# Transposes of probabilities two groups behind the scores, and a weight's conversion in three successive steps

## The chip, the core and the metric

The kernel runs on one core of a Trainium2 chip. The core has a matrix engine (TensorE, PE in the profile), a vector engine (DVE), an activation engine (ACT), GpSimd (POOL) and a queue engine that issues transfers (SyncE, SP). Each has its own queue of instructions, whose order is fixed when the program is built. The metric is the device time of one execution in microseconds, less is better.

## The reference

Attention over a window and a few sink positions, then two feed-forward blocks on its output.

```python
scores = scale * np.matmul(q, k.transpose(0, 1, 3, 2))       # q, k, v: (2, 8, 768, 64)
keep = is_sink | in_window                                   # 4 sinks, window of 128
a = softmax(np.where(keep, scores, -1000000000.0))
x = np.matmul(a, v)                                          # -> (1536, 512)
...
x = (silu(x @ w_gate) * (x @ w_val)) @ w_out                 # 512 -> 1536 -> 512
h = x @ w_in
return (np.maximum(h, 0) + alpha * np.minimum(h, 0)) @ w_out2   # 512 -> 2048 -> 512
```

The weights come as 64-bit floats, everything else that is large as 32-bit floats.

## The kernel before

Attention works on 24 groups. A group is a pair of heads and two blocks of 128 query rows. For a group there are these stages (class Group):

- prep (L213): PE transposes keys and queries, ACT copies them to `th`.
- scores (L248): four matmuls into `ps_s`, a masked pass with row maximum on DVE (L271, from the first group with sink columns on with a copy before it, L269), four exponentials on ACT (L275) that also add up the row sums.
- norm (L288): `rinv`, two small DVE operations (L291, L292), then POOL multiplies the probabilities `pr` by it (L298).
- flip (L310): PE transposes the probabilities into `ps_p` (L320), ACT or DVE copies them to `pt`.
- values (L336): PE multiplies with v into `xp` (L351), ACT and DVE split the result into a high part `xh` (L847) and a low part `xl` (L848), which the first feed-forward block reads.

The function attention (L376) writes the stages of different groups one behind the other. In iteration x it writes scores of group x, values of x - 2, flip of x - 1, norm of x, prep of x + 2, and the loads of x + 3. After each piece it yields a cost.

The feed-forward products need 32-bit weights as a high and a low part. The class Stream loads raw weights (L559, three buffers) and converts them, one at a call of tick (L609). A conversion (L574) is a copy on ACT into `w_m` (L587), three bit operations on DVE (L589, L592, L595), the high part `wh` on ACT (L604) and the low part `wl` = `w_m` - `wh` on DVE (L605).

The function fast (L817) drives both. Until 8 groups have their values it ticks once after each flip, up to six weights. After that, for every 2300 of summed cost, it runs one piece of the first feed-forward block on the first 512 rows and ticks once. Twelve weights have room while attention runs.

The order on DVE during attention is the order in which the program is written. The order on PE, ACT, POOL and SyncE is made by a scheduler from its own estimate of times, so moving a stage in attention moves instructions on all of them.

```python
for x in range(n + 2):
    if x < n:
        for t in range(NG):
            groups[x].scores(t)
    if x >= 2:
        for c in groups[x - 2].values():
            yield c, None
```

Of the kernel before, what the change touches and what calls it, by code (L numbers as in the profile page):

```python
# [7 lines left out]
F32 = mybir.dt.float32  # L8
# [3 lines left out]
AF = mybir.ActivationFunctionType  # L12
ALU = mybir.AluOpType
# [3 lines left out]
P = 128  # L17
# [3 lines left out]
KD = DM // P  # L21
# [14 lines left out]
WX = 7  # L36
RB = 3
VB = 3
ORDER = ((0, 3), (1, 2), (4, 5))
EARLY = 6  # L40
WEAVE = 2300
# [98 lines left out]
class Group:  # L140
    def __init__(self, nc, g, q, k, v, b, hp, i0, put, cs, blk):
        self.nc, self.g, self.q, self.k, self.v = nc, g, q, k, v
        self.b, self.hp, self.i0, self.put = b, hp, i0, put
        self.cs, self.blk = cs, blk
        self.h0 = 2 * hp
        self.j0 = max(0, i0 - 1)
        self.nk = i0 + NG - self.j0
        self.sink = i0 + NG > 2
        self.off = 1 if i0 == 0 else 0
        self.before = self.lead = None  # L150
        if self.sink:
            self.kpos = [0, P, P + KW]
            self.spos = 2 * P
            self.qpos = [P + 2 * KW, P + 3 * KW]
        else:
            self.kpos = [0, P]
            self.qpos = [2 * P, 3 * P]
# [35 lines left out]
    def load_v(self):  # L193
        nc, p = self.nc, self.g.raw_p
        b, h0, j0, nk = self.b, self.h0, self.j0, self.nk
        if self.i0 == 0:
            self.vt = self.wide(self.v, "vr", VB) if self.lead is None else self.lead.vt
            o = 0 if self.lead is None else 2
            self.vr = [[self.vt[:, t, o + e] for e in range(2)] for t in range(nk)]
            return  # L200
        vr = p.tile([P, NG, 4, D], F32, tag="vr", name="vr", bufs=VB).rearrange("p t h d -> p (t h d)")
        vr = vr[:, :NK * 2 * D].rearrange("p (t e d) -> p t e d", e=2, d=D)
# [173 lines left out]
def attention(groups, begin):  # L376
    n = len(groups)

    def stage(f, x):
        if x < n:  # L380
            return getattr(groups[x], f)()

    stage("load", 0)
    begin[0]()
    stage("load_v", 0)
    stage("load", 1)
    stage("load", 2)
    begin[1]()
    for x in range(2):
        for c in groups[x].prep():  # L390
            yield c, None
    for x in range(n + 2):
        if x < n:
            for t in range(NG):
                groups[x].scores(t)
            yield 1200, None
        if x >= 2:
            for c in groups[x - 2].values():
                yield c, None
            yield 0, groups[x - 2]  # L400
        if 1 <= x <= n:
            for t in range(NG):
                groups[x - 1].flip(t)
            yield 1000, None
        if x < n:
            groups[x].norm()
            yield 0, None
        if x + 2 < n:
            for c in groups[x + 2].prep():
                yield c, None  # L410
        stage("load", x + 3)
        stage("load_v", x + 1)
        if x in (2, 4):
            begin[2](x // 2 - 1)
# [131 lines left out]
def big(g, dt, name):  # L546
    return g.x_p.tile([P, KD, T], dt, tag="x", name=name)


class Stream:  # L550
    def __init__(self, nc, g, seq):
        self.nc, self.g, self.seq = nc, g, seq
        self.n_load = self.n_conv = self.n_done = 0
        self.raw, self.w, self.home = {}, {}, {}

    def room(self):
# [14 lines left out]
        self.raw[i] = raw  # L571
        self.n_load += 1

    def convert(self):  # L574
        nc, g, i = self.nc, self.g, self.n_conv
        kind, src, f, scale, slot = self.seq[i]
        rv = self.raw.pop(i).rearrange("p (c t) -> p c t", t=2)
        lo, hi = rv[:, :, 0], rv[:, :, 1]
        m = g.raw_w.tile([P, KD * P], F32, tag="m", name="w_m")
        mi, mu = m.bitcast(I32), m.bitcast(U32)  # L580
        if slot is None or g.exact:
            nc.scalar.activation(m, hi.bitcast(F32), AF.Copy, scale=scale)
            nc.vector.tensor_scalar(out=m, in0=m, scalar1=WMAX, scalar2=-WMAX, op0=ALU.min, op1=ALU.max)
            w2 = g.w2_p.tile([P, KD * P], F32, tag="w2", name="w_2")
            sign, wi = mi, w2.bitcast(I32)
        else:
            nc.scalar.activation(m, hi.bitcast(F32), AF.Abs, scale=scale, accum_out=g.wsum[:, slot:slot + 1])  # L587
            sign, wi = hi, mi
        nc.vector.tensor_scalar(  # L589
            out=wi, in0=mi, scalar1=3, scalar2=0x7FFFFFF8, op0=ALU.logical_shift_left, op1=ALU.bitwise_and  # L590
        )
        nc.vector.scalar_tensor_tensor(  # L592
            out=mi, in0=sign, scalar=-(2**31), in1=wi, op0=ALU.bitwise_and, op1=ALU.bitwise_or
        )
        nc.vector.scalar_tensor_tensor(  # L595
            out=mu, in0=lo.bitcast(U32), scalar=29, in1=mu, op0=ALU.logical_shift_right, op1=ALU.bitwise_or
        )
        w32 = m
        home = next(h for h in g.w_ps if h[1])
        home[1] -= 1  # L600
        self.home[i] = home
        wh = home[0].tile([P, KD * P], F32R, tag="wh", name="wh")
        wl = home[0].tile([P, KD * P], F32R, tag="wl", name="wl")
        nc.scalar.activation(wh, w32, AF.Copy)  # L604
        nc.vector.tensor_tensor(out=wl, in0=w32, in1=wh, op=ALU.subtract)  # L605
        self.w[i] = (wh, wl)
        self.n_conv += 1

    def tick(self, ahead=RB):  # L609
        n = len(self.seq)  # L610
        if self.n_conv < n and self.room() and self.n_load > self.n_conv:
            self.convert()
        while self.n_load < n and self.n_load < self.n_conv + ahead:
            self.load()

    def get(self, i):
        while self.n_conv <= i:
            assert self.room(), (i, self.n_conv, self.n_done)
            if self.n_load <= self.n_conv:
                self.load()  # L620
            self.convert()
        return self.w[i]

    def done(self, n=1):
# [186 lines left out]
def moe(nc, g, st, xs, out, halves):  # L811
    ys = []
    m1 = Moe1(nc, g, st, 0, xs, lambda *y: ys.append(y))
    return m1, Moe2(nc, g, st, 3 * NF1, ys, out, halves)


def fast(nc, tc, ctx, g, n_sink, window, alpha, q, k, v, w_gate, w_val, w_out, x2_in, x2_out, out):  # L817
# [4 lines left out]
    xs = [(big(g, F32R, "xh"), big(g, F32R, "xl")) for _ in range(NPASS)]  # L822
    m1, m2 = moe(nc, g, st, xs, out, [[blk * NG * P for blk in pair] for pair in ORDER])

# [14 lines left out]
    with ExitStack() as inner:  # L839
# [3 lines left out]
        def put(n, half):  # L843
            xh, xl = xs[n]

            def split(src, hp, ts):
                nc.scalar.activation(xh[:, hp, ts], src, AF.Copy)  # L847
                nc.vector.tensor_tensor(out=xl[:, hp, ts], in0=src, in1=xh[:, hp, ts], op=ALU.subtract)  # L848

            return split  # L850

        groups = [
            Group(nc, g, q, k, v, blk // 3, hp, NG * (blk % 3), put(n, half), BLKS[half], blk)
            for n, pair in enumerate(ORDER) for hp in range(NPAIR) for half, blk in enumerate(pair)
        ]
# [89 lines left out]
```

## Time and profile before

| what | value |
|---|---|
| median of three runs | 693.28 us (691.6 to 694.32) |
| the profiled execution's own time | 694.07 us |
| its span, first to last instruction | 692.3 us |
| TensorE busy | 663.5 us, 96% |
| DVE busy | 409.4 us, 59% |
| ACT busy | 302.6 us, 44% |
| POOL busy | 43.0 us, 6% |
| chain of work that ended last, by engine | PE 85%, DVE 5%, ACT 3% |

The span is what the trace covers; the 1.8 us that the execution's own time has beyond it lie around it. Busy shares are averages over the whole span: attention and the feed-forward blocks load the engines differently, so the stretches have to be read one at a time. A number in brackets at the end of a timeline row is the time that the engine stood idle just before this instruction, with what released it.

### The profile page before, as it was taken

The numbers are of one execution on the slowest core, as the hardware profiler recorded it, in microseconds if no ns is written. First come the engines' busy times: TensorE is split into PE (matmuls) and PEld (weight loads), VectorE is DVE, ScalarE is ACT, GpSimd is POOL, SyncE is SP. The second block draws the span as 40 slices with busy tenths as digits, with TensorE's granted clock in tenths as the row PEclk, the third lists the DMA queues.
The fourth block names the chain that finished last, engine by engine and source line by source line (L and its number), as shares of the span: only waits on it lengthen the run. The fifth ranks groups of instructions, "written<-read, shape, count | busy, mean of one in ns | idle before, by whom it ended". The sixth has DMA issues, their size and how long they took to land.

```text
span 692.3 us, 8940 instructions
## 1 busy us (share of the span) xinstructions
PE 663.5 (96%) x3195; PEld 529.6 (76%) x3195; DVE 409.4 (59%) x925; ACT 302.6 (44%) x686; POOL 43.0 (6%) x82
## 2 busy tenths in 40 slices
PE   5769999999999999999999999999999999999996
PEld 2547767677678888888888888888888888888885
DVE  4677778855569862279642489537933753333432
ACT  4877545667356631155322356436611532113320
POOL 2232013311200000000000000000000000000000
PEclk9879999999999999999999999999999999999999
DMA  8764444421025540025400033301500000000111
GB/s 163 172 182 109 121 138 109 101 57 24 12 62 181 183 153 0 1 61 183 123 0 1 0 122 121 123 1 46 167 30 1 1 0 1 0 1 1 61 62 65
DMA packets 76276, 50.87 MB, mean 73 GB/s; under 512 B 50624, under 2 KB 71104, under 8 KB 76224
## 3 DMA queue, kind: packets, MB, share of 16 engines
q1 hardware_dynamic: 73872, 50.22, 25.5%
q8 instruction: 27, 0.44, 0.3%
q10 hardware_dynamic: 2352, 0.01, 0.2%
q14 instruction: 25, 0.20, 0.1%
HBM read 47.07 MB, written 3.15 MB: 73 GB/s over the span
## 4 chain that ended last, share of the span: by engine, by line
PE 85%; DVE 5%; ACT 3%; SPq 3%; issue 1%; DMA 1%; POOL 1%; DVEq 0%; ACTq 0%; POOLq 0%
PE ph L657 6%; PE pf L781 6%; PE ph L655 6%; PE pf L779 6%; PE pf L780 6%; PE ph L656 6%; PE po L723 5%; PE po L725 5%; PE po L724 5%; PE pg L655 4%; PE pv L655 4%; PE pg L656 4%; PE pg L657 4%; PE pv L657 4%; PE pv L656 4%; PE xp L351 2%
## 5 line engine op out<-in xcount | busy, mean ns | idle before, releaser
L668 ACT ACTIVATE hh<-hid 128x512 fp32r<-128x512 f32 x84 | 52.9, 630 | 66.4 <-DVE hid L707 37.2
L669 DVE TENSOR_TENSOR hl<-hid,hh 128x512 fp32r<-128x512 f32 x84 | 57.9, 689 | 35.0 <-ACT hh L668 34.8
L655 PE MATMUL ph<-yh,wh 128*128 128x512 f32 x192 | 74.8, 389 | 0.0
L657 PE MATMUL ph<-yh,wl 128*128 128x512 f32 x192 | 74.7, 389 | 0.0
L656 PE MATMUL ph<-yl,wh 128*128 128x512 f32 x192 | 74.7, 389 | 0.0
L779 PE MATMUL pf<-wh,hh 128*128 128x512 f32 x192 | 74.7, 389 | 0.0
L780 PE MATMUL pf<-wl,hh 128*128 128x512 f32 x192 | 74.7, 389 | 0.0
L761 ACT ACTIVATE neg<-ph,sal 128x512 f32<-128x512 f32 x48 | 33.0, 687 | 93.4 <-PE ph L657 93.4
L781 PE MATMUL pf<-wh,hl 128*128 128x512 f32 x192 | 72.1, 389 | 0.0
L604 ACT ACTIVATE wh<-w_m 128x512 fp32r<-128x512 f32 x68 | 42.6, 630 | 57.3 <-DVE w_m L595 16.9
L605 DVE TENSOR_TENSOR wl<-w_m,wh 128x512 fp32r<-128x512 f32 x68 | 46.4, 687 | 34.8 <-ACT wh L604 34.8
L763 DVE SCALAR_TENSOR_TENSOR hid<-ph,sig,neg 128x512 f32<-128x512 f32 x48 | 36.0, 749 | 38.4 <-ACT neg L761 38.0
L655 PE MATMUL pg<-xh,wh 128*128 128x512 f32 x144 | 56.8, 397 | 0.0
L723 PE MATMUL po<-hh,wh 128*128 128x512 f32 x144 | 56.7, 396 | 0.0
L655 PE MATMUL pv<-xh,wh 128*128 128x512 f32 x144 | 56.5, 392 | 0.0
L657 PE MATMUL pv<-xh,wl 128*128 128x512 f32 x144 | 56.1, 389 | 0.0
L656 PE MATMUL pv<-xl,wh 128*128 128x512 f32 x144 | 56.0, 389 | 0.0
L656 PE MATMUL pg<-xl,wh 128*128 128x512 f32 x144 | 56.0, 390 | 0.0
L657 PE MATMUL pg<-xh,wl 128*128 128x512 f32 x144 | 56.0, 390 | 0.0
L724 PE MATMUL po<-hh,wl 128*128 128x512 f32 x144 | 55.9, 389 | 0.0
L786 DVE TENSOR_TENSOR acc<-pf,acc 128x512 f32<-128x512 f32 x36 | 23.2, 686 | 52.0 <-PE pf L781 52.0
L725 PE MATMUL po<-hl,wh 128*128 128x512 f32 x144 | 52.4, 391 | 0.0
(122 smaller groups left out, 1203.5 us busy)
## 6 DMA issues: line engine op xcount, KB each, us to landing
w_raw<-in_moe_w_out SPq DMA_DIRECT2D x28, 512.0 KB, 3.3
w_raw<-in_moe_w_in SPq DMA_DIRECT2D x16, 512.0 KB, 3.8
w_raw<-in_moe_w_gate SPq DMA_DIRECT2D x12, 512.0 KB, 3.8
w_raw<-in_moe_w_val SPq DMA_DIRECT2D x12, 512.0 KB, 4.4
vr<-in_v SPq DMA_DIRECT2D x32, 96.0 KB, 2.2
out<-acc SPq DMA_DIRECT2D x12, 256.0 KB, 2.3
qr<-in_q SPq DMA_DIRECT2D x32, 64.0 KB, 2.2
kr<-in_k SPq DMA_DIRECT2D x16, 96.0 KB, 2.2
```

Source lines behind the costliest of these rows:

```text
L605: nc.vector.tensor_tensor(out=wl, in0=w32, in1=wh, op=ALU.subtract)
L655: nc.tensor.matmul(ps, wh[:, c], xh[:, kk], start=(kk == 0), stop=False)
L656: nc.tensor.matmul(ps, wh[:, c], xl[:, kk], start=False, stop=False)
L657: nc.tensor.matmul(ps, wl[:, c], xh[:, kk], start=False, stop=(kk == KD - 1))
L668: nc.scalar.activation(hh, hid, AF.Copy)
L669: nc.vector.tensor_tensor(out=hl, in0=hid, in1=hh, op=ALU.subtract)
L723: nc.tensor.matmul(ps, wh[:, mc], hh, start=(x == 0), stop=False)
L724: nc.tensor.matmul(ps, wl[:, mc], hh, start=False, stop=False)
L725: nc.tensor.matmul(ps, wh[:, mc], hl, start=False, stop=(x == CHUNK - 1))
L779: nc.tensor.matmul(ps, hh[:, ts], wh, start=(x == 0), stop=False)
L780: nc.tensor.matmul(ps, hh[:, ts], wl, start=False, stop=False)
L781: nc.tensor.matmul(ps, hl[:, ts], wh, start=False, stop=(x == CHUNK - 1))
```

## The change

The distance between scores and flip becomes a constant, LAG = 2 in place of 1. In iteration x the program now writes scores of group x, values of x - 3, flip of x - 2, norm of x, prep of x + 2. The conversion is cut in three: start (the copy on ACT), bits (the three bit operations and wh), low (wl). One tick does low of one weight, bits of the next and start of the one after it. A weight is counted as converted when its bits are written, and can be used when low is written.

```diff
--- before.py
+++ after.py
@@ -36,6 +36,7 @@
 WX = 7
 RB = 3
 VB = 3
+LAG = 2
 ORDER = ((0, 3), (1, 2), (4, 5))
 EARLY = 6
 WEAVE = 2300
@@ -389,18 +390,18 @@
     for x in range(2):
         for c in groups[x].prep():
             yield c, None
-    for x in range(n + 2):
+    for x in range(n + LAG + 1):
         if x < n:
             for t in range(NG):
                 groups[x].scores(t)
             yield 1200, None
-        if x >= 2:
-            for c in groups[x - 2].values():
+        if x > LAG:
+            for c in groups[x - LAG - 1].values():
                 yield c, None
-            yield 0, groups[x - 2]
-        if 1 <= x <= n:
+            yield 0, groups[x - LAG - 1]
+        if LAG <= x < n + LAG:
             for t in range(NG):
-                groups[x - 1].flip(t)
+                groups[x - LAG].flip(t)
             yield 1000, None
         if x < n:
             groups[x].norm()
@@ -550,7 +551,8 @@
 class Stream:
     def __init__(self, nc, g, seq):
         self.nc, self.g, self.seq = nc, g, seq
-        self.n_load = self.n_conv = self.n_done = 0
+        self.n_load = self.n_start = self.n_conv = self.n_done = 0
+        self.begun = self.halves = None
         self.raw, self.w, self.home = {}, {}, {}
 
     def room(self):
@@ -571,20 +573,30 @@
         self.raw[i] = raw
         self.n_load += 1
 
-    def convert(self):
-        nc, g, i = self.nc, self.g, self.n_conv
+    def start(self):
+        nc, g, i = self.nc, self.g, self.n_start
         kind, src, f, scale, slot = self.seq[i]
         rv = self.raw.pop(i).rearrange("p (c t) -> p c t", t=2)
+        hi = rv[:, :, 1].bitcast(F32)
+        m = g.raw_w.tile([P, KD * P], F32, tag="m", name="w_m")
+        if slot is None or g.exact:
+            nc.scalar.activation(m, hi, AF.Copy, scale=scale)
+        else:
+            nc.scalar.activation(m, hi, AF.Abs, scale=scale, accum_out=g.wsum[:, slot:slot + 1])
+        self.begun = (i, rv, m)
+        self.n_start += 1
+
+    def bits(self):
+        nc, g = self.nc, self.g
+        (i, rv, m), self.begun = self.begun, None
+        kind, src, f, scale, slot = self.seq[i]
         lo, hi = rv[:, :, 0], rv[:, :, 1]
-        m = g.raw_w.tile([P, KD * P], F32, tag="m", name="w_m")
         mi, mu = m.bitcast(I32), m.bitcast(U32)
         if slot is None or g.exact:
-            nc.scalar.activation(m, hi.bitcast(F32), AF.Copy, scale=scale)
             nc.vector.tensor_scalar(out=m, in0=m, scalar1=WMAX, scalar2=-WMAX, op0=ALU.min, op1=ALU.max)
             w2 = g.w2_p.tile([P, KD * P], F32, tag="w2", name="w_2")
             sign, wi = mi, w2.bitcast(I32)
         else:
-            nc.scalar.activation(m, hi.bitcast(F32), AF.Abs, scale=scale, accum_out=g.wsum[:, slot:slot + 1])
             sign, wi = hi, mi
         nc.vector.tensor_scalar(
             out=wi, in0=mi, scalar1=3, scalar2=0x7FFFFFF8, op0=ALU.logical_shift_left, op1=ALU.bitwise_and
@@ -595,30 +607,40 @@
         nc.vector.scalar_tensor_tensor(
             out=mu, in0=lo.bitcast(U32), scalar=29, in1=mu, op0=ALU.logical_shift_right, op1=ALU.bitwise_or
         )
-        w32 = m
         home = next(h for h in g.w_ps if h[1])
         home[1] -= 1
         self.home[i] = home
         wh = home[0].tile([P, KD * P], F32R, tag="wh", name="wh")
         wl = home[0].tile([P, KD * P], F32R, tag="wl", name="wl")
-        nc.scalar.activation(wh, w32, AF.Copy)
-        nc.vector.tensor_tensor(out=wl, in0=w32, in1=wh, op=ALU.subtract)
+        nc.scalar.activation(wh, m, AF.Copy)
+        self.halves = (i, m, wh, wl)
+        self.n_conv += 1
+
+    def low(self):
+        (i, m, wh, wl), self.halves = self.halves, None
+        self.nc.vector.tensor_tensor(out=wl, in0=m, in1=wh, op=ALU.subtract)
         self.w[i] = (wh, wl)
-        self.n_conv += 1
+
+    def step(self):
+        if self.halves:
+            self.low()
+        if self.begun and self.room():
+            self.bits()
+        if not self.begun and self.n_load > self.n_start:
+            self.start()
 
     def tick(self, ahead=RB):
         n = len(self.seq)
-        if self.n_conv < n and self.room() and self.n_load > self.n_conv:
-            self.convert()
+        self.step()
         while self.n_load < n and self.n_load < self.n_conv + ahead:
             self.load()
 
     def get(self, i):
-        while self.n_conv <= i:
-            assert self.room(), (i, self.n_conv, self.n_done)
-            if self.n_load <= self.n_conv:
+        while i not in self.w:
+            assert self.halves or self.room(), (i, self.n_conv, self.n_done)
+            if self.n_load <= self.n_start:
                 self.load()
-            self.convert()
+            self.step()
         return self.w[i]
 
     def done(self, n=1):
```

Three places show how the written order moves. First DVE, from the low part of group 4's result to the next `rinv`; `xl` is the low part of a group's result, `w_m` the weight in work, `rinv` the reciprocal of the row sums. Before, wl_586 belongs to the weight just worked on:

```order
L848 TENSOR_TENSOR xl_91<-xp_562,xh_90 128x256
L589 TENSOR_SCALAR w_m_580<-w_m_580 128x512
L592 SCALAR_TENSOR_TENSOR w_m_580<-w_raw_459,w_m_580 128x512
L595 SCALAR_TENSOR_TENSOR w_m_580<-w_raw_459,w_m_580 128x512
L605 TENSOR_TENSOR wl_586<-w_m_580,wh_585 128x512
L291 TENSOR_SCALAR rinv_591<-ssum_544 128x4
L292 RECIPROCAL rinv_591<-rinv_591 128x4
```

After the change wl_535 belongs to the weight of the tick before, w_m_472, and stands ahead of the bits of w_m_537:

```order
L870 TENSOR_TENSOR xl_91<-xp_581,xh_90 128x256
L621 TENSOR_TENSOR wl_535<-w_m_472,wh_534 128x512
L601 TENSOR_SCALAR w_m_537<-w_m_537 128x512
L604 SCALAR_TENSOR_TENSOR w_m_537<-w_raw_418,w_m_537 128x512
L607 SCALAR_TENSOR_TENSOR w_m_537<-w_raw_418,w_m_537 128x512
L292 TENSOR_SCALAR rinv_610<-ssum_563 128x4
L293 RECIPROCAL rinv_610<-rinv_610 128x4
```

The operations are the same; wl has moved from behind the bits of its own weight to ahead of the bits of the next.

Second PE, one iteration early in the program: scores of group 5 (`ps_s`), values (`xp`), transposes of probabilities (`ps_p` from `pr`), transposes of queries and keys (`ps_k`). Before, xp_494 is group 3's and pr_415 group 4's:

```order
L265 MATMUL ps_s_478<-th_398 128x128
L265 MATMUL ps_s_479<-th_398 128x128
L265 MATMUL ps_s_486<-th_398 128x256
L265 MATMUL ps_s_487<-th_398 128x256
L351 MATMUL xp_494<-pt_439,vr_276 64x256 x2
L351 MATMUL xp_494<-pt_439,vr_276 64x128 x2
L320 MATMUL ps_p_502<-ident_61,pr_415 128x128 x2
L320 MATMUL ps_p_506<-ident_61,pr_415 128x128 x4
L229 MATMUL ps_k_529<-ident_61,kr_405 128x128 x2
L229 MATMUL ps_k_529<-ident_61,qr_408 128x128 x2
```

After the change xp_453 is group 2's and pr_316 group 3's:

```order
L266 MATMUL ps_s_437<-th_358 128x128
L266 MATMUL ps_s_438<-th_358 128x128
L266 MATMUL ps_s_445<-th_358 128x256
L266 MATMUL ps_s_446<-th_358 128x256
L352 MATMUL xp_453<-pt_399,vr_263 64x256 x2
L352 MATMUL xp_453<-pt_399,vr_263 64x128 x2
L321 MATMUL ps_p_461<-ident_61,pr_316 128x128 x2
L321 MATMUL ps_p_465<-ident_61,pr_316 128x128 x4
L230 MATMUL ps_k_480<-ident_61,kr_365 128x128 x2
L230 MATMUL ps_k_480<-ident_61,qr_368 128x128 x2
```

Within an iteration the stages keep their places; values and transposes of probabilities belong to groups one further back.

Third SyncE's queue near the start, where `w_raw` is the first raw weight, and kr, qr and vr are loads of the third pair of groups. Before:

```order
L367 DMA ksr_180<-in_k 128x1x64 x2
L567 DMA w_raw_256<-in_moe_w_gate 128x4x256
L162 DMA kr_270<-in_k 128x4x64 x2
L162 DMA qr_273<-in_q 128x4x64 x2
L162 DMA vr_276<-in_v 128x4x64 x2
L567 DMA w_raw_324<-in_moe_w_gate 128x4x256
```

After the change:

```order
L368 DMA ksr_180<-in_k 128x1x64 x2
L163 DMA kr_257<-in_k 128x4x64 x2
L163 DMA qr_260<-in_q 128x4x64 x2
L163 DMA vr_263<-in_v 128x4x64 x2
L569 DMA w_raw_295<-in_moe_w_gate 128x4x256
L163 DMA vr_371<-in_v 128x4x64 x2
```

The first weight's load has moved behind the six loads of the third pair.

## Rows read from the trace of the kernel before

**Rows 1.** The page, busy time of each engine, share of the span, instructions

```profile
PE 663.5 (96%) x3195; PEld 529.6 (76%) x3195; DVE 409.4 (59%) x925; ACT 302.6 (44%) x686; POOL 43.0 (6%) x82
```

**Rows 2.** Stretches of 20 us: busy time and instructions of each engine, PEclk, DMA share, GB/s

```profile
0.00:20.00 20.00, 11.78 (x67) 7.02 (x67) 9.52 (x57) 10.28 (x35) 5.55 (x14) 1.00 0.92 186
20.00:40.00 20.00, 13.22 (x77) 8.47 (x77) 14.53 (x48) 14.77 (x50) 5.18 (x7) 0.78 0.71 170
40.00:60.00 20.00, 16.40 (x95) 10.35 (x96) 13.72 (x52) 15.15 (x49) 5.95 (x11) 0.79 0.54 137
```

**Rows 3.** Timeline of PE: start, us, line op out<-in, idle before and releaser

```profile
38.09 0.69 PE L320 MATMUL ps_p<-ident,pr 128*128 128x128 f32 x2 [2.93 <-POOL pr L298]
...
39.08 1.11 PE L320 MATMUL ps_p<-ident,pr 128*128 128x128 f32 x4 [0.31 <-POOL pr L298]
...
44.08 0.69 PE L320 MATMUL ps_p<-ident,pr 128*128 128x128 f32 x2
...
58.60 1.24 PE L265 MATMUL ps_s<-th 64*128 64x288 f32 x8
...
60.57 0.50 PE L655 MATMUL pg<-xh,wh 128*128 128x512 f32 x1
```

**Rows 4.** Waits, 0 to 62 us: engine, line, releaser, us, times, longest

```profile
PE ps_p L320 <- POOL pr L298: 10.9, 11, 2.9
...
DVE wl L605 <- ACT wh L604: 7.7, 6, 2.0
```

**Rows 5.** Timeline of DVE, one step (group 4's rinv to group 5's)

```profile
36.87 0.16 DVE L291 TENSOR_SCALAR rinv<-ssum 128x4 f32<-128x4 f32 x1
...
38.37 0.42 DVE L848 TENSOR_TENSOR xl<-xp,xh 128x256 fp32r<-128x256 f32 x1
...
38.70 0.61 DVE L589 TENSOR_SCALAR w_m<-w_m 128x512 int32<-128x512 int32 x1
...
42.24 0.69 DVE L605 TENSOR_TENSOR wl<-w_m,wh 128x512 fp32r<-128x512 f32 x1 [1.47 <-ACT wh L604]
...
42.85 0.18 DVE L291 TENSOR_SCALAR rinv<-ssum 128x4 f32<-128x4 f32 x1
```

**Rows 6.** Timeline of DVE, rinv of groups 1, 7, 8, and group 8's scores' end

```profile
16.43 0.17 DVE L291 TENSOR_SCALAR rinv<-ssum 128x4 f32<-128x4 f32 x1 [1.82 <-ACT pr L275]
...
55.22 0.16 DVE L291 TENSOR_SCALAR rinv<-ssum 128x4 f32<-128x4 f32 x1
...
57.92 0.42 DVE L848 TENSOR_TENSOR xl<-xp,xh 128x256 fp32r<-128x256 f32 x1
...
59.23 0.17 DVE L291 TENSOR_SCALAR rinv<-ssum 128x4 f32<-128x4 f32 x1 [0.90 <-ACT pr L275]
```

**Rows 7.** Timeline of ACT: first weight's start, then one step

```profile
14.73 0.67 ACT L587 ACTIVATE w_m<-w_raw 128x512 f32<-128x512 f32 x1 [0.29 <-DMA w_raw<-in_moe_w_gate]
...
30.69 0.67 ACT L587 ACTIVATE w_m<-w_raw 128x512 f32<-128x512 f32 x1 [1.82 <-DMA w_raw<-in_moe_w_val]
...
31.35 0.35 ACT L275 ACTIVATE pr<-ps_s,nb 128x128 f32<-128x128 f32 x1
...
33.94 0.64 ACT L234 ACTIVATE th<-ps_k 128x512 f32<-128x512 f32 x1
...
35.60 0.63 ACT L604 ACTIVATE wh<-w_m 128x512 fp32r<-128x512 f32 x1 [1.02 <-DVE w_m L595]
```

**Rows 8.** Timeline of SyncE's queue: issues of the first two weights

```profile
10.24 0.47 SPq L567 DMA_DIRECT2D w_raw<-in_moe_w_gate  x1
...
15.15 0.51 SPq L567 DMA_DIRECT2D w_raw<-in_moe_w_gate  x1
```

**Rows 9.** Waits, 62 to 205 us

```profile
DVE wl L605 <- ACT wh L604: 5.5, 6, 2.0
```

**Rows 10.** Groups by line: count, busy us, mean ns, idle before

```profile
L699 ACT ACT_TABLE_LOAD x6 | 7.7, 1283 | 0.1
```

**Rows 11.** Stretch of 5 us, columns as in group 2

```profile
40.00:45.00 5.00, 4.76 (x23) 2.64 (x22) 3.38 (x15) 2.56 (x6) 1.86 (x3) 0.51 0.56 150
```

## Prediction

> **What bounds the kernel now.** I read the busy times first, then stretches of 20 us, then the waits of the worst stretches, then the queues one by one. TensorE is busy 663.5 us of a span of 692.3 us [rows 1], so all that can be won without taking work from it is 28.8 us. The stretches show where that lies: 8.2, 6.8 and 3.6 us of the first three times 20 us [rows 2], together 18.6 us. From about 60 us on the engine hardly stops, and nothing that the change moves behind that point can save much. So the question is when the first product with a weight starts: at 60.57 us [rows 3].
>
> In the first 62 us PE waits 10.9 us, in 11 waits, for POOL's normalized probabilities [rows 4]. But POOL is only the last link. It waits for rinv, and rinv stands on DVE, in order, behind a whole weight conversion. I call the time from one group's rinv to the next a step. Between rinv of group 4 (36.87) and of group 5 (42.85) DVE does rinv and the four score passes (1.50 us to xl), xl (0.33), the three bit operations (38.70 until the wait that ends at 42.24, less 1.47 of waiting: 40.77, so 2.07 us) and wl (0.61) [rows 5]. That is 4.51 us of work and 1.47 us of waiting for wh, 5.98 us in all. From rinv of group 1 (16.43) to that of group 8 (59.23) seven steps take 42.8 us, 6.11 each [rows 6]. DVE waits 7.7 us for wh here in all [rows 4].
>
> **The change, part by part.** But for two table loads (below) no instruction is added: work moves, and two waits go.
>
> Transposes one group later: the transposes that PE meets in a step belong to a group whose normalization was queued a step before. POOL has then had a whole step for it, so I set PE's 10.9 us of waits to nothing; what is late next is the engine that paces the step. It costs one more step ahead of the first weight product, since values of group 7 now come in step 10 and not in step 9.
>
> Conversion in three steps: wl is emitted a tick after wh, so DVE no longer stands (1.47 us in the step above) for ACT within the conversion. A step is then paced by the fuller of two queues. DVE: 4.51 us with both wl and bits, 1.50 + 0.33 + 2.07 = 3.90 with bits alone. From group 8 on, where the sink columns come in, rinv to xl takes 55.22 to 57.92 = 2.70 us [rows 6] in place of 1.50, so 5.71 us. ACT: the exponentials, xh and the two copies of transposed probabilities take 31.35 to 33.94 = 2.59 us, th 0.64, wh 0.63, the start of a conversion 31.35 - 30.69 = 0.66: 4.52 us with all, 3.9 without one of the last two [rows 7].
>
> The first weight's load moves too. In SyncE's queue it now stands behind six more loads of the third pair; today those six lie between the issues at 10.24 and 15.15, so I place its issue at 14.6 [rows 8]. Today ACT takes it up at 14.73, 4.5 us after the issue, having waited 0.29 [rows 7]; then 19.1 after the change. Group 1 is rid of that start (16.43 - 0.95 = 15.5), and group 2 gets it in the middle of its exponentials: 19.1 + 0.66 + about 1.1 for the rest (somewhat under half of ACT's 2.59) gives rinv at 20.9, a step of 5.4 us.
>
> The steps by these sums, as the new order on DVE hands out the weights: group 2 5.4; groups 3 to 6 3.9 each; group 7 4.5; groups 8 and 9 5.7. Sum 36.9, so rinv of group 9 at 15.5 + 36.9 = 52.4. Today the first weight product follows rinv of group 8 by 60.57 - 59.23 = 1.34 us. After the change rinv has wl and bits (2.7 us) ahead of it that this product doesn't wait for, so it starts between 51.1 and 53.7. I take 53.0, near the upper end, because two in-order queues that feed each other never pack fully. At worst each of eight steps keeps half of the 1.47 us wait: 5.9 us more, 58.9. **Gain 7.6 us (1.7 to 9.5).**
>
> Work already done: at that moment PE also has the scores of group 10 behind it, about 1.2 us [rows 3]. It is work that no longer stands in the full stretch: **gain 1.2 us**.
>
> Weights converted late: by then four weights are finished and a fifth has its bits, against six today, so 1.5 x (2.07 + 0.61) = 4.0 us of DVE work moves behind the start of the products, where PE is full and DVE busy too. Against it, the waits of wl for wh in that later part, 5.5 us in six waits [rows 9], go the same way as above. Between 1.5 us gained and 4.0 lost; the waits are nearly the size of the work, so I take 0.8 lost.
>
> Table loads: the order lists 16 loads of an activation table on ACT in place of 14; a silu of the feed-forward block now comes between two halves of a group's exponentials. A load takes 1.283 us, and the six at the product's own line had 0.1 us of idle time before them in all [rows 10]. Two cost 2.6 us of ACT, hidden where ACT has room: between 0 and 2.6; ACT is not the fullest engine there, so 0.4 lost. The Trainium skill, "ScalarE: Activation LUTs", section "What ACT_TABLE_LOAD costs", puts a switch at about 2.66 us, a drain of 1.38 us included; the rows show no such drain. By its figure the two would be 5.3 us of ACT and the sum could be up to 2.7 us worse, which no end of my range uses.
>
> The three-step conversion in the later, full part of the kernel: PE has no stops there to take away, and the conversions run several weights ahead. Nothing; if that cover were gone, PE would wait there as it does for nothing now, and stretches after 60 us would show it.
>
> Sum: -7.6 - 1.2 + 0.8 + 0.4 = -7.6 us. Against the profiled execution (694.07 us with what lies around the span) that is 686.5; that run stood 0.8 above the median of the three shown, 693.28, which would give 685.7. **I predict 686.0 us.** The ends of the terms give 694.07 - 9.5 - 1.2 - 1.5 = 681.9 and 694.07 - 1.7 - 1.2 + 4.0 + 2.6 = 697.8.
>
> **The rivals.**
>
> Starts that wait for their load (no change). A conversion's start now stands among a group's exponentials, one tick before its bits, so every raw weight is wanted earlier. Today one start waited 1.82 us for its transfer, and the exponentials queued behind it waited as well [rows 7]. If the five others do so, 5 x 1.82 = 9.1 us comes back: 695.1. Against it: the other start in those rows waited 0.29 only, and weights are issued several steps ahead.
>
> TensorE at half speed (slower). The granted clock is 0.51 from 40 to 45 us, near the lower of its two levels (1.2 and 2.4 GHz), after PE had stood 2.93 us before 38.09 [rows 3, 11]. At that clock one step of PE, from group to group, runs from 38.09 to 44.08, 5.99 us with 0.31 of waiting in it, so 5.7 us of work [rows 3], more than DVE or ACT need. If short stops in every step keep the clock down, PE paces the start: at 6.0 us a step the first product comes at 15.5 + 8 x 6.0 + 1.34 = 64.8, which gives 694.07 + 4.3 - 1.2 + 1.2 = 698.4. It decides from a step of (60.57 - 1.34 - 15.5) / 8 = 5.5 us. Against it: that stop was a wait for POOL, and POOL's waits go. The Trainium skill, "TensorE: Matmul & The Clock Gate", section "Part 1: The HAM clock gate", says that the slow clock is the default and activity lifts it; the trace agrees as far as the 0.51 after that stop.
>
> Late weights in the full part: PE waits where today it does not. The price is in the sum with 4.0 us at most, so alone it leaves 689.2, still faster.
>
> **How the numbers follow.** The forecast 0.73, the starts that wait 0.19, half speed 0.08. A measurement of this kernel tells about 0.5% from no change, so faster is below 689.8 and slower above 696.7. The range 681.9 to 694.0 holds nearly all of the forecast and about half of the waiting starts (those where not all five wait); it leaves out half speed, 0.08, and the other half, 0.10. Of the chances: faster 0.73, same 0.19, slower 0.08.
>
> **What would show it.** Right: PE's wait for POOL is under 2 us in the first 62 us; DVE's wait of wl for wh is gone; steps of 4 to 5.7 us; the first weight product near 53 us; later stretches of 20 us as full as now. Wrong: a first weight product after 59 us; a clock near 0.5 through the start; waits of ACT for raw weights of 5 us or more; or several us of new PE waits between 60 and 100 us.

## The result: 687.22 us in place of 693.5 us, and the profile after

The changed kernel took **687.22 us** (median of 4 runs, 687.01 to 688.01), the kernel before, measured beside it, 693.5 us (4 runs, 691.6 to 694.32): a ratio of 0.9915 with a 95% interval from 0.9893 to 0.9937. The profiled execution took 687.25 us (before 694.07) with a span of 685.5 us (before 692.3). A second measurement, below, found a smaller gain: 0.9946, 0.9932 to 0.9959. It is faster in both, each time by under 2%.

The page of the changed kernel, busy time of each engine [rows 1]:

```profile
PE 658.3 (96%) x3195; PEld 527.1 (77%) x3195; DVE 408.5 (60%) x925; ACT 303.8 (44%) x688; POOL 44.9 (7%) x82
```

Of the 6.8 us that the span lost, 5.2 are PE's busy time (663.5 - 658.3) and only 1.6 its idle time (28.8 to 27.2), with the same 3195 instructions. That looks as if PE's work had become cheaper rather than its stops fewer; the filling experiment below says how this is to be read.

Stretches of the changed kernel, columns as in [rows 2]:

```profile
20.00:40.00 20.00, 16.63 (x118) 11.05 (x117) 12.79 (x58) 16.79 (x60) 7.26 (x12) 0.91 0.60 139
40.00:60.00 20.00, 17.67 (x109) 12.18 (x106) 19.16 (x67) 16.96 (x59) 8.09 (x13) 1.00 0.72 183
30.00:35.00 5.00, 5.00 (x34) 3.41 (x32) 2.39 (x10) 2.82 (x11) 1.76 (x3) 0.66 0.38 84
```

From 40 to 60 us DVE now works 19.16 of 20 us (13.72 before): it is nearly full and sets the pace. The granted clock is full but for one piece, 30 to 35 us.

Waits of the changed kernel, 0 to 62 us, two of PE's [rows 4]:

```profile
PE ps_ks L373 <- DMA ksr<-in_k: 2.4, 1, 2.4
...
PEld ps_p L321 <- POOL pr L299: 0.7, 3, 0.3
```

The 10.9 us of PE's waits for POOL are gone; what is left is 0.7 us of PEld, PE's weight load. DVE's wait of wl for wh is gone too. A wait for the second batch's sink keys (ksr) is new.

DVE's timeline after the change: rinv of group 1, a wait for xh between rinv of group 3 and group 4, rinv of groups 4 and 5, one step (group 6's rinv to group 7's), rinv of group 9 [rows 5, 6]:

```profile
15.37 0.17 DVE L292 TENSOR_SCALAR rinv<-ssum 128x4 f32<-128x4 f32 x1 [0.77 <-ACT pr L276]
...
27.34 0.42 DVE L870 TENSOR_TENSOR xl<-xp,xh 128x256 fp32r<-128x256 f32 x1 [1.16 <-ACT xh L869]
...
29.47 0.16 DVE L292 TENSOR_SCALAR rinv<-ssum 128x4 f32<-128x4 f32 x1
...
35.36 0.17 DVE L292 TENSOR_SCALAR rinv<-ssum 128x4 f32<-128x4 f32 x1 [1.82 <-ACT pr L276]
...
39.18 0.16 DVE L292 TENSOR_SCALAR rinv<-ssum 128x4 f32<-128x4 f32 x1
...
41.21 0.96 DVE L621 TENSOR_TENSOR wl<-w_m,wh 128x512 fp32r<-128x512 f32 x1
42.09 0.41 DVE L601 TENSOR_SCALAR w_m<-w_m 128x512 int32<-128x512 int32 x1
...
43.88 0.16 DVE L292 TENSOR_SCALAR rinv<-ssum 128x4 f32<-128x4 f32 x1
...
54.73 0.16 DVE L292 TENSOR_SCALAR rinv<-ssum 128x4 f32<-128x4 f32 x1
```

wl stands ahead of the bits of the next weight and waits for nothing: 4.70 us with all of it, where [rows 5] had 5.98. Eight steps take 54.73 - 15.37 = 39.36 us, 4.92 each (6.11 before).

PE's timeline after the change: the stop for ksr, the first weight product, the largest wait for a late weight [rows 3]:

```profile
29.49 0.30 PE L373 MATMUL ps_ks<-ident,ksr 128*128 128x128 f32 x1 [2.38 <-DMA ksr<-in_k]
...
53.30 0.50 PE L677 MATMUL pg<-xh,wh 128*128 128x512 f32 x1
...
93.15 0.50 PE L746 MATMUL po<-hh,wl 128*128 128x512 f32 x1 [0.87 <-DVE wl L621]
```

The first product comes 7.27 us earlier (60.57 before). Behind it the span has 632.2 us, before 631.7.

ACT's timeline after the change: the first weight's start, and a table load between a conversion and an exponential [rows 7, 10]:

```profile
18.49 0.66 ACT L585 ACTIVATE w_m<-w_raw 128x512 f32<-128x512 f32 x1 [0.89 <-DMA w_raw<-in_moe_w_gate]
...
74.45 0.63 ACT L615 ACTIVATE wh<-w_m 128x512 fp32r<-128x512 f32 x1 [0.42 <-DVE w_m L607]
75.13 1.28 ACT L276 ACT_TABLE_LOAD   x1
76.42 0.40 ACT L276 ACTIVATE pr<-ps_s,nb 128x160 f32<-128x160 f32 x1
```

### The profile page after: what moved, and what is told of

Its sections match the earlier page's. It is cut to its first block, busy times and chain, and to the rows that moved or that the text cites. A ratio compares the mean times of both kernels' runs of the same rounds, so it can differ in the third digit from the quotient of the medians.

```text
span 685.5 us, 8954 instructions
## 1 busy us (share of the span) xinstructions
PE 658.3 (96%) x3195; PEld 527.1 (77%) x3195; DVE 408.5 (60%) x925; ACT 303.8 (44%) x688; POOL 44.9 (7%) x82
## 4 chain that ended last, share of the span: by engine, by line
PE 84%; DVE 3%; ACT 2%; issue 1%; DVEq 0%; ACTq 0%
PE ph L678 6%; PE ph L679 6%; PE pf L802 6%; PE pf L803 6%; PE pf L801 6%; PE ph L677 6%; PE po L746 4%; PE po L747 4%; PE po L745 4%; PE pv L677 4%; PE pg L677 4%; PE pg L678 4%; PE pg L679 4%; PE pv L679 4%; PE pv L678 4%; PE xp L352 2%
```

## The experiments

Three theories of the gain stood against each other: both edits are needed, the lag alone does it, the split conversion alone does it. The kernel before was run beside each of the kernels below: on one chip for the lag alone, the three steps alone, the sink keys and the early weight (median 694.03 us), on a second for the two single cuts, the filling and the end of attention (694.49 us), on a third for the last three (693.65 us). Across chips the ratios are compared, not the times.

### The lag alone

```diff
--- the kernel before
+LAG = 2
...
-    for x in range(n + 2):
+    for x in range(n + LAG + 1):
...
-        if x >= 2:
-            for c in groups[x - 2].values():
+        if x > LAG:
+            for c in groups[x - LAG - 1].values():
...
-        if 1 <= x <= n:
+        if LAG <= x < n + LAG:
             for t in range(NG):
-                groups[x - 1].flip(t)
+                groups[x - LAG].flip(t)
```

> The kernel before with LAG = 2 alone; a weight is still converted in one piece. Theory (both parts are needed, because the pace of a step is set by DVE and ACT and not by POOL): PE's waits for POOL's probabilities in the first 62 us fall from 10.9 us to under 2, but DVE's wait of wl for wh stays at 6 to 9 us, the steps shorten to 5.3 to 6.0 us at best, and one step more is needed before the first weight product, so that product starts at 58 to 65 us (60.57 before, 53.30 after the change) and the time is 690 to 697 us. Rival (POOL's answer was the limit, and the lag alone brings the gain): first weight product before 55 us, time 686 to 688.5 us.

Measured: 695.74 us, ratio 1.0027 (1.0013 to 1.0040). Two waits in the first 62 us, then rinv of group 1, one wl and rinv of group 9, then the first product:

```profile
DVE wl L606 <- ACT wh L605: 8.9, 6, 3.6
PE ps_ks L373 <- DMA ksr<-in_k: 3.6, 1, 3.6
```

```profile
15.44 0.17 DVE L292 TENSOR_SCALAR rinv<-ssum 128x4 f32<-128x4 f32 x1 [0.77 <-ACT pr L276]
...
35.91 0.69 DVE L606 TENSOR_TENSOR wl<-w_m,wh 128x512 fp32r<-128x512 f32 x1 [3.59 <-ACT wh L605]
...
63.71 0.17 DVE L292 TENSOR_SCALAR rinv<-ssum 128x4 f32<-128x4 f32 x1 [0.34 <-ACT pr L276]
```

```profile
63.90 0.50 PE L656 MATMUL pg<-xh,wh 128*128 128x512 f32 x1
```

PE has no wait for POOL left, and it is worth nothing here: eight steps of 6.03 us in place of seven of 6.11, and the first product 3.3 us later. This kernel is 0.27% slower, about 1.9 us.

Not all of that is the price of one more step. PE stands 3.61 us for ksr, the values behind that stop come late, ACT waits 3.41 us for them with xh and wh queued, and wl's longest wait, 3.59 us in a step of 8.09 us (group 3's rinv to group 4's), is the end of this chain. So the stop for ksr stands in the 8.9 us, in the 6.03 and in the time. The other five waits of wl, 5.3 us together, come without it.

### The conversion in three steps alone

```diff
--- the changed kernel
-LAG = 2
+LAG = 1
```

> The changed kernel with LAG = 1: the conversion in three steps alone. Theory (both parts are needed): DVE's wait of wl for wh in the first 62 us goes from 7.7 us to under 1, but PE keeps waiting for POOL, 6 to 12 us; the steps shorten by about half of the 1.47 us wait, the first weight product starts at 55 to 58 us, and the time is 688.5 to 691.5 us. Rival (the standing wl was the whole cause, the lag is not needed): steps of 4 to 5 us, first weight product at 52 to 54 us, time 686 to 688.5 us. Second rival (POOL's chain through rinv, POOL and the transposes sets the pace whatever DVE does): first product after 59 us, time over 691.5 us.

Measured: 685.54 us (684.61 to 685.98), ratio 0.9874 (0.9855 to 0.9894), better than the whole change. PE's wait for POOL, rinv of groups 1 and 8, first product:

```profile
PE ps_p L321 <- POOL pr L299: 5.7, 8, 1.7
```

```profile
16.03 0.17 DVE L292 TENSOR_SCALAR rinv<-ssum 128x4 f32<-128x4 f32 x1 [1.42 <-ACT pr L276]
...
50.53 0.18 DVE L292 TENSOR_SCALAR rinv<-ssum 128x4 f32<-128x4 f32 x1
```

```profile
50.42 0.50 PE L677 MATMUL pg<-xh,wh 128*128 128x512 f32 x1
```

My theory falls here, and the first rival holds, with a first product still earlier than it said and a time 0.5 us below its range. PE still waits 5.7 us for POOL in eight stops, yet the steps are 4.93 us ((50.53 - 16.03) / 7), as long as with the lag. PE has room for those stops in a step that DVE and ACT pace.

### Which of the two cuts in the conversion

Low apart (LAG = 1; start, bits and wh in one tick, wl in the next):

```diff
--- three steps, LAG = 1
     def step(self):
         if self.halves:
             self.low()
-        if self.begun and self.room():
-            self.bits()
-        if not self.begun and self.n_load > self.n_start:
-            self.start()
+        if self.room() and self.n_load > self.n_start:
+            self.start()
+            self.bits()
...
```

> LAG = 1, and of the three steps only the last stands apart: a tick does low of one weight, then start and bits of the next one together. Theory (what the three steps win is that wl no longer stands in DVE's queue for wh): the wait of wl in the first 62 us is under 1 us (7.7 before), the first weight product starts at 50 to 52.5 us (50.42 with all three steps and LAG = 1), time 685.0 to 687.0 us. Rival (the copy on ACT must be there a tick ahead, or DVE stands for w_m in place of wh): new waits of DVE for the start of 3 us or more, first product after 54 us, time over 688.5 us.

Start apart (LAG = 1; bits, wh and wl in one tick, start in the one before):

```diff
--- three steps, LAG = 1
     def step(self):
-        if self.halves:
-            self.low()
         if self.begun and self.room():
             self.bits()
+            self.low()
...
```

> LAG = 1, and of the three steps only the first stands apart: a tick does bits and low of one weight together, then start of the next one. Theory (the standing wl is the loss): DVE keeps waiting 6 to 9 us for wh in the first 62 us, steps near 6 us, first weight product at 57 to 61 us, time 690.5 to 694.5 us. Rival (the early start is what wins): wait of wl halved or less, first product before 54 us, time under 688.5 us.

Measured: low apart 684.7 us, ratio 0.9857 (0.9840 to 0.9874); start apart 695.11 us, ratio 1.0011 (1.0000 to 1.0022). With low apart, PE's wait for POOL, rinv of groups 1 and 8, and the first product:

```profile
PE ps_p L321 <- POOL pr L299: 4.0, 7, 1.1
```

```profile
16.10 0.17 DVE L292 TENSOR_SCALAR rinv<-ssum 128x4 f32<-128x4 f32 x1 [1.42 <-ACT pr L276]
...
51.21 0.17 DVE L292 TENSOR_SCALAR rinv<-ssum 128x4 f32<-128x4 f32 x1 [0.96 <-ACT pr L276]
```

```profile
52.45 0.50 PE L676 MATMUL pg<-xh,wh 128*128 128x512 f32 x1
```

With start apart, DVE's wait, rinv of groups 1 and 8, and the first product:

```profile
DVE wl L621 <- ACT wh L615: 4.9, 5, 1.6
```

```profile
17.05 0.17 DVE L292 TENSOR_SCALAR rinv<-ssum 128x4 f32<-128x4 f32 x1 [2.41 <-ACT pr L276]
...
60.02 0.17 DVE L292 TENSOR_SCALAR rinv<-ssum 128x4 f32<-128x4 f32 x1
```

```profile
58.40 0.50 PE L676 MATMUL pg<-xh,wh 128*128 128x512 f32 x1
```

The whole gain lies in one move, wl a tick behind its wh. Low apart has steps of 5.02 us and no wait of wl; start apart has steps of 6.14 us. Start apart waits less for wh than I expected (4.9, not 6 to 9 us), and its steps are none the shorter; its time is 0.6 us above my range, that of low apart 0.3 us below. All three steps with LAG = 1 (0.9874) and low apart (0.9857) can't be told apart.

Another reading would be that less conversion work stands ahead of the first product. The traces speak against it. The kernel before reaches that product with the bits and wl of six weights done, low apart with six bits and five wl: one wl less, 0.61 us, against a first product 8.1 us earlier. Start apart has moved more of it behind the product (five bits and four wl are done, as with three steps), and gains nothing: its first product is 2.2 us earlier, and in the profiled execution, the slowest of its twelve, PE then stands 7.7 us up to 200 us, where it stood 4.2 us before.

### Filling PE's waits

```diff
--- the kernel before, in flip
         ps = g.ps_t.tile([P, 512], F32, tag="ps", name="ps_p")
+        if t == 0 and not self.sink:
+            for x in range(12):
+                nc.tensor.transpose(ps[:, x % 4 * P:(x % 4 + 1) * P], g.ident, g.ident)
```

> The kernel before with 12 transposes of the identity written into ps_p ahead of the transposes of probabilities, for each of the first eight groups; they fill part of PE's waits for POOL and are overwritten. Nothing else is changed. Theory (DVE's queue with its standing wl sets the pace; PE's clock doesn't): the granted clock from 20 to 60 us rises from 0.78 and 0.79 to over 0.9, PE's waits for POOL fall by half or more, DVE's wait of wl for wh stays at 6 to 9 us, the first weight product stays between 59.5 and 62 us, time 692.5 to 695.5 us. Rival (the half clock between 20 and 60 us was what made the steps long): first product before 56 us, time under 690 us.

Measured: 694.73 us, ratio 0.9998 (0.9986 to 1.0009). Stretches of this kernel, columns as above:

```profile
20.00:40.00 20.00, 16.76 (x120) 12.00 (x119) 13.87 (x47) 14.39 (x50) 5.13 (x7) 0.91 0.68 170
40.00:60.00 20.00, 18.43 (x146) 13.50 (x145) 16.32 (x63) 17.22 (x59) 8.05 (x15) 1.00 0.59 152
```

Its waits in the first 62 us, and its first product:

```profile
DVE wl L608 <- ACT wh L607: 4.8, 6, 1.2
PE ps_p L323 <- POOL pr L298: 4.4, 7, 1.3
```

```profile
58.55 0.50 PE L658 MATMUL pg<-xh,wh 128*128 128x512 f32 x1
```

The clock rises as far as the change raised it, 0.91 and 1.00, and the time does not move. The first product comes 2.0 us earlier than before, 1 us outside what I expected, and the wait of wl falls to 4.8 us, below the 6 to 9 expected, so the steps are a little shorter (5.85 us), but the median of twelve runs doesn't show it. So the 5.2 us of busy time that the changed kernel saves are not the cause of its gain: a clock as high as the changed kernel's comes here with 2.0 us of its 7.3 at the first product, and with nothing that the time shows. Most of what PE did more slowly before was done in time in which it would have stood anyway. The filling transposes take time of PE themselves; what they may cost is not separated. The Trainium skill, "TensorE: Matmul & The Clock Gate", section "Part 1: The HAM clock gate", says that the slow clock is the default and that activity releases it. The trace agrees: 96 transposes that compute nothing lift the clock from 0.78 and 0.79.

### The new wait for sink keys

```diff
--- the changed kernel
-        if x in (2, 4):
-            begin[2](x // 2 - 1)
+        if x in (2, 10):
+            begin[2](x // 8)
```

> The changed kernel with the second batch's sink keys transposed in iteration 10 and not in iteration 4, the loads where they were. In the changed kernel PE stands 2.38 us at 29.49 for that load of sink keys (ksr), and its clock falls to 0.66 from 30 to 35 us. Theory (the wait of PE, which works in order, delays every step behind it): the wait is gone, the step of group 5 falls from 5.89 us to about 4, the clock stays at 1.00 from 30 to 35 us, the first weight product comes 1.5 to 2.5 us earlier than 53.30, and the time falls by 1.5 to 2.5 us, to 684.7 to 685.7 us. Rival (DVE or ACT or the raw weights' loads pace that step anyway): first product within 0.5 us of 53.30, time 686.7 to 687.7 us.

Measured: 685.98 us, ratio 0.9884 (0.9864 to 0.9904). The stretch from 30 to 35 us, and the first product:

```profile
30.00:35.00 5.00, 3.75 (x30) 2.58 (x28) 3.65 (x20) 5.00 (x18) 3.06 (x6) 1.00 0.46 104
```

```profile
51.09 0.50 PE L677 MATMUL pg<-xh,wh 128*128 128x512 f32 x1
```

The step of group 5 falls to 33.82 - 29.84 = 3.98 us and the first product comes 2.2 us earlier, as the theory said. The time is 0.3 us above the theory's range. Against the changed kernel 1.2 us show by the medians and 2.1 by the ratios (0.9915 - 0.9884 = 0.0031 of 693.5); the intervals overlap, so of the gain only the place is shown, not its size.

This run also comes nearest to a price of the lag without the stop. On the same chip three steps with LAG = 1 took 685.54 us (0.9874) and this kernel, which is three steps with LAG = 2 and no wait for ksr, 685.98 us (0.9884): 0.4 us, with intervals that overlap. Its steps are 4.69 us ((52.89 - 15.37) / 8), somewhat shorter than the 4.93 with LAG = 1, and the one step more takes that back: the first product comes 0.7 us later (51.09, 50.42).

### One weight more, converted early

```diff
--- the changed kernel
-                    st.tick(1 + (done > 1))
+                    st.tick(2)
```

> The changed kernel with two raw weights asked for at each early tick from the first on, so that the second weight is loaded with the first and every conversion of the early part stands one tick earlier: five weights whole and a sixth with its bits at the first weight product, in place of four and a fifth. Theory (weights converted late cost about what the forecast put on them, 0.8 us, and the price of converting one more early is a fuller DVE in one more step, 0.6 us): first weight product at 53.3 to 54.5 us, PE's two waits for wl at 83.31 and 93.15 (1.1 us together) gone, time within 0.7 us of the changed kernel, 686.5 to 687.9 us. Rival (late weights are what the later stretches lost, 1.7 us): time 685.0 to 686.2 us.

Measured: 688.62 us, above both ranges, with a ratio of 0.9917 (0.9899 to 0.9935) that is the changed kernel's own. ACT's timeline, two starts in the step of group 2:

```profile
19.15 0.68 ACT L585 ACTIVATE w_m<-w_raw 128x512 f32<-128x512 f32 x1 [1.11 <-DMA w_raw<-in_moe_w_gate]
...
20.72 0.66 ACT L585 ACTIVATE w_m<-w_raw 128x512 f32<-128x512 f32 x1 [0.35 <-DMA w_raw<-in_moe_w_gate]
```

Here the first rival of the prediction does happen: two starts wait 1.46 us for their loads with the exponentials queued behind them, group 2's step is 6.73 us (5.09 in the changed kernel), and the first product comes at 56.31. Behind the first product the span is 631.0 us against 632.2: the earlier weight earns 1.2 us and its place costs 3.0. PE's two waits for wl behind the first product are gone, as expected.

### Transposes ahead of the values at the end

```diff
--- three steps, LAG = 1
+        if n <= x < n + LAG:
+            for t in range(NG):
+                groups[x - LAG].flip(t)
+            yield 1000, None
...
-        if LAG <= x < n + LAG:
+        if LAG <= x < n:
```

> The conversion in three steps with LAG = 1, and in the last iterations, where no scores are left, the transposes of probabilities written ahead of the values. Theory (PE's two gaps at the end of attention, 0.35 and 1.05 us waiting for DVE's copies pt, are time of their own, since PE is the full engine there): the gap of the last group shrinks or goes and the time falls by 0.5 to 1.4 us against LAG = 1 with the values first, which took 685.54 us: 684.1 to 685.0 us. Rival (the gap only moves, to xp of the group before or to the first product that reads its result): 685.2 to 686.0 us.

Measured: 687.32 us, ratio 0.9892 (0.9872 to 0.9911); no gain over 0.9874, and above the ranges of theory and rival. PE's timeline of this kernel, the new stop and two products after it; then the stretch behind the stop; then, of the kernel with the values first, one of the two gaps and a product after it:

```profile
181.42 0.66 PE L321 MATMUL ps_p<-ident,pr 128*128 128x128 f32 x4 [2.55 <-POOL pr L308]
...
183.42 0.63 PE L750 MATMUL po<-hh,wl 128*128 128x512 f32 x1
...
186.90 0.40 PE L750 MATMUL po<-hh,wl 128*128 128x512 f32 x1
```

```profile
182.90:186.40 3.50, 3.50 (x10) 2.73 (x9) 0.29 (x1) 0.00 (x0) 0.00 (x0) 0.52 0.00 0
```

```profile
179.12 1.09 PE L352 MATMUL xp<-pt,vr 128*64 128x256 f32 x12 [1.10 <-ACT pts L335]
...
180.92 0.39 PE L746 MATMUL po<-hh,wl 128*128 128x512 f32 x1
```

The last group's transposes now stand for POOL, 2.55 us in place of gaps of 1.10 and 1.05, and for the next 3.5 us the granted clock is 0.52: a product takes 0.63 us and not 0.40. Here PE is the full engine, so stop and slow clock are both paid: by an estimate 0.4 us for the longer stop (2.55 - 1.10 - 1.05) and 1.7 us for the clock (3.5 x 0.48), of 2.4 us by which the span behind the first product is longer. Another 0.9 us by which the profiled executions differ stand ahead of the first product (51.33, 50.42), where the order on PE is the same in both: so much two executions can differ there by themselves.

### The changed kernel and two others on one chip

The changed kernel once more (its diff stands above), low apart with LAG = 2, and low apart with LAG = 1:

> The changed kernel itself once more (LAG = 2, three steps), on the same chip as the two kernels below. Theory (the later transposes cost one step of DVE's pace, and win nothing): 687 to 688 us here, ratio to the kernel before 0.990 to 0.993, and 1.5 to 3 us above LAG = 1 with low apart. Rival (what looked like the price of the lag was a difference of chips): within 0.7 us of it.

> LAG = 2 with only low apart (start and bits in one tick). Theory (the lag costs the same whatever the steps are): first weight product 1.5 to 3.5 us later than with LAG = 1 (52.45), at 54 to 56 us, time 686.0 to 688.0 us. Rival (with start and bits in one tick DVE leans more on ACT, and the lag gives it room): time under 685 us.

> LAG = 1 with only low apart, the fastest so far (684.7 us), on the same chip as the changed kernel. Theory: ratio to the kernel before 0.984 to 0.988, below the changed kernel by 1.5 to 3 us, with intervals that don't meet or barely so. Rival (a chip's difference): within 0.7 us of the changed kernel.

Measured: the changed kernel 689.82 us (687.27 to 690.65), ratio 0.9946 (0.9932 to 0.9959); low apart with LAG = 2 686.59 us, 0.9892 (0.9877 to 0.9907); with LAG = 1 **684.02 us** (683.75 to 684.29), 0.9859 (0.9843 to 0.9874). First products of the last two, one kernel each:

```profile
57.34 0.50 PE L676 MATMUL pg<-xh,wh 128*128 128x512 f32 x1
```

```profile
51.76 0.50 PE L676 MATMUL pg<-xh,wh 128*128 128x512 f32 x1
```

Between the two of low apart, which ran on one chip, the lag costs 2.6 us, and their intervals don't meet. With LAG = 2 PE waits for ksr here too, for a shorter time:

```profile
PE ps_ks L373 <- DMA ksr<-in_k: 1.3, 1, 1.3
```

The first product of LAG = 2 came later than I expected (57.34, not 54 to 56). Of the 5.6 us between the two first products half is made up behind them: 627.8 us against 630.7. The changed kernel lies outside what I expected for it (687 to 688 us, 0.990 to 0.993), and 5.8 us above the fastest one here, more than the 1.5 to 3 I expected. Its profiled execution was the fastest of its five (687.27 us, first product at 53.35), so where the other four lost 1.8 to 3.4 us is not seen. The three slowest had a mean granted clock of 0.990 to 0.992, the fastest 0.997; what lowered it there stays open.

## Why the prediction came out right, and which step of it was wrong

All kernels that settle the cause, in one table; a step is the mean from rinv to rinv of group 1 to 8 (LAG = 1) or 9, and the wait is PE's for ksr in the first 62 us:

| conversion | LAG | wait for ksr, us | step, us | first product, us | span behind it, us | ratio |
|---|---|---|---|---|---|---|
| whole (before) | 1 | 0 | 6.11 | 60.57 | 631.7 | 1 |
| whole | 2 | 3.6 | 6.03 | 63.90 | 630.3 | 1.0027 |
| start apart | 1 | 0 | 6.14 | 58.40 | 636.3 | 1.0011 |
| three steps | 1 | 0 | 4.93 | 50.42 | 632.3 | 0.9874 |
| three steps (the change) | 2 | 2.4 | 4.92 | 53.30 | 632.2 | 0.9915, 0.9946 |
| three steps, sink keys moved | 2 | 0 | 4.69 | 51.09 | 632.8 | 0.9884 |
| low apart | 1 | 0 | 5.02, 4.92 | 52.45, 51.76 | 630.5, 630.7 | 0.9857, 0.9859 |
| low apart | 2 | 1.3 | 5.16 | 57.34 | 627.8 | 0.9892 |

**The mechanism was right for DVE.** A step is paced by DVE and ACT, and the standing wl was what made it long: with wl a tick later the step is 4.7 to 5.2 us, without that 6.0 to 6.1, whatever the lag.

**The step that failed is the one on the transposes.** The prediction set PE's 10.9 us of waits for POOL to nothing, which was so, and took that as part of the way to shorter steps, with one more step as its price. The waits were nearly all slack: taking them away with the lag alone left the step at 6.03 us, and leaving 5.7 us of them left it at 4.93, where 4.69 is the shortest with the lag. What remained was the price, and it is not one number: 1.9 us with the old conversion, with a stop of 3.6 us for ksr in it; 2.6 us with low apart, with a stop of 1.3 us; 0.4 us with three steps and the sink keys moved, where the intervals overlap. So no run shows that the lag wins anything, and how much of its price is the extra step and how much the stop for ksr stays open. Summing both edits together, the prediction could not see that one of them won nothing. A sum for each edit alone, with its own count of steps, would have asked the question.

**The sum of the steps was short.** Forecast 36.9 us, measured 39.36. Group 2 was 5.09 (5.4), group 7 4.70 (4.5), groups 8 and 9 5.42 and 5.43 (5.7 each). The miss lies in groups 4 and 5, 4.91 and 5.89 where 3.9 each stood. In group 4's step DVE stands 1.16 us for ACT's xh (the row at 27.34), in a step that the sum took as full of work. Group 5's excess is the wait for ksr, which the prediction did not look at. PE waits for that load in every kernel with LAG = 2 and the sink keys in their place, and in none with LAG = 1: its issue on SyncE's queue, at 24.69 us before and 24.64 with three steps and LAG = 1, has moved to 26.47 in the changed kernel and to 28.40 with the lag alone. The first product at 53.30 (53.0) is right through a second error: it came 1.43 us ahead of rinv of group 9, where I had put it 0.6 behind. Two terms of about 2 us cancelled, which was luck.

**Behind the first product** the sum had -1.2 for group 10's scores, +0.8 for late weights and +0.4 for table loads, together nothing; measured is +0.5 (632.2 - 631.7). Its parts differ, though. PE's idle time from the first product to 200 us, the changed kernel:

```profile
53.30:200.00 146.70, 140.29 (x831) 105.53 (x830) 105.20 (x321) 90.30 (x245) 25.42 (x46) 1.00 0.33 88
```

and the kernel before:

```profile
60.57:200.00 139.43, 135.27 (x813) 101.24 (x812) 95.69 (x309) 80.74 (x231) 25.80 (x51) 1.00 0.30 76
```

Idle are 6.41 and 4.16 us, so 2.25 us more. Late weights are 1.1 us of PE's waits (0.87 in the row at 93.15). With three steps and LAG = 1, as many weights late, PE is idle 4.27 us from its first product to 200 us, and with the lag alone 5.83: the lag brings about 2 us of later stops, a term that the prediction did not have.

**Table loads:** two more (the trace has 14 and 12 of them), each 1.28 us with the next operation right behind it, and PE is busy 20.00 of the 20 us from 60 to 80, where the two added ones stand; nothing of the 0.4 is seen. The Trainium skill, "ScalarE: Activation LUTs", section "What ACT_TABLE_LOAD costs", counts a drain of 1.38 us with each; the row at 75.13 follows a copy that ended at 75.08, so no drain shows here either.

**The rivals.** Starts that wait for their load: one, 0.89 us, in the changed kernel; the experiment with one weight more early shows that it was near. Half clock: one stretch of 0.66, and by the filling experiment the clock by itself is worth nothing that the time shows. Late weights: 1.1 us.

The time, -6.3 us by medians against -7.6 by the sum, is a sum mis-sized by 1.3 us in the first measurement. In the second the kernel took 689.82 us, 3.8 less than the kernel before: inside the range, but half of the sum, and at the edge of what a measurement tells from no change.

## What to carry to other kernels

Before crediting the longest wait on the fullest engine, ask what paces the loop: a wait of PE that fits into a step set by DVE and ACT is slack, and 10.9 us of it were worth nothing here. In an in-order queue, an operation that needs another engine's answer to the operation just ahead of it is better written one round later, behind other work; one tick of distance for one subtraction gave all of the gain. Price each edit of a change alone, with its own cost (here one more round in flight), and look which load the new order makes late: the stop for ksr came with the lag, whether the steps got shorter or not.

## What the runs showed of the hardware

PE's busy time depends on its clock, so busy time can fall by 5 us with the same instructions and not be what made a kernel faster. At the full stretch, a stop of 2.55 us was followed by 3.5 us at a clock of 0.52, while the stops of 1.10 and 1.05 us in the kernel that it was made from were followed by products of 0.39 to 0.40 us, the full-clock time. The changed kernel took 687.22 and 689.82 us in two measurements in which the kernel before took 693.5 and 693.65; whether chips or runs make that difference is open.
